# Agent attention with a gated convolution: one DMA transpose for a pair of units, and shifted rows copied as sixteen and three single rows

## The chip, the cores and the metric

The kernel runs on one core of a Trainium2 chip. A core has the engines PE (matmuls; its weight loads are listed as PEld), DVE, ACT and POOL (element-wise work), and SP, which here issues nearly all DMA transfers. Each engine executes its own instructions in order and waits on semaphores for the others. All transfers of the core are served by 16 DMA engines. The metric is the device time of one execution in microseconds (us); lower is better. The profile is of one execution and gives its span, from the first to the last instruction.

## The reference, cut to what matters

```python
# q, k, v: (4, 12800, 128); agents: (4, 49, 128)
def sm(a, b):                                   # row softmax of the scaled scores
    s = (a @ b.transpose(0, 2, 1)) / np.sqrt(128)
    e = np.exp(s - s.max(-1, keepdims=True))
    return e / (e.sum(-1, keepdims=True) + 1e-09)

x = sm(q, agents) @ (sm(agents, k) @ v)         # attention through 49 agents

gate_pre = sum(conv_w[t] * x_delayed_by(4 - t) for t in range(5))   # causal, per channel
gate = 1 / (1 + exp(-gate_pre))
out = (gate * (x @ w_val)) @ w_out
```

## The kernel before, in words

Each of the four batches has 12800 positions. They are worked in *units* of 1280 positions (10 a batch, 40 in all, numbered g) for keys, values and queries, and in *chunks* of 512 (25 a batch, 100 in all) for the gate, the value path and the output. Two units, an even one and the odd one behind it, make a *segment* of 2560 positions, which is five chunks. So there are 20 segments.

Keys and values of a batch give 49 agent values. `fold_weights` folds them into the convolution and value weights, so that gate and value of a chunk come out of matmuls whose contracted axis is the agents and whose moving operand is the softmax weights of the queries (`queries`), one row for each agent.

The softmax weights are held in 16 bits. To keep accuracy they are stored as rows of three kinds in `pt` (line 220), a tile of 128 positions by 10 blocks by 128 columns: 49 columns with the low part, 49 with the high part, and 30 that repeat the high part of two out of every three of the first 45 agents; these 30 meet the residuals of the folded weights. `queries` writes `pt` with ACT (line 779), POOL (line 784, the 30 repeated columns) and POOL again (line 794, the low parts). There are four `pt` tiles, used in turn.

A unit's `pt` has positions on partitions; the matmuls need agents there. `transposes` (line 827) turns it into one half of `x1`, a tile of 128 rows by one segment (four of them, with a few columns ahead of it that `halo`, line 813, copies from the segment before on POOL). The first four units are transposed on PE; the other 36 by one DMA transpose each, issued by SP (line 835).

The residuals of the 19 agents that are not repeated in `pt` need their high parts at all five delays. They are held in `x2` (line 222, three tiles): 19 agents by 5 delays are 95 rows, row by row a copy of an `x1` row shifted by 0 to 4 columns. `shifts` (line 866) makes these copies by two DMA transfers (line 884), cut by `X2CUTS` (line 36): 15 source rows, every third, to 75 rows of `x2`, and 4 neighbouring source rows to 20 more. The first four units have such copies each for themselves; from the fifth on they are made once for a segment, when both halves of `x1` are there. So there are 22 groups of copies, 44 transfers.

A chunk's gate (`gates`, line 898) is five matmuls on `x1` at five column offsets (line 922) and one on the 95 rows of `x2` (line 926), all into one accumulator, then a tanh on ACT. Its value (`values`, line 942) is one matmul on `x1` (line 949) and one on `x2` (line 953); then come the product on DVE (line 962) and its split into two 16-bit halves, `hh` on ACT and `hl` on POOL (line 973). `project` (line 979) has three matmuls (lines 992 to 994), the last of which needs `hl`, a scaled copy on ACT and the store.

Loads go through 11 buffers `ld` in the order of use, so they run ahead as far as buffers are free.

The order of the work is made in two ways. PE's sequence is written out by hand: the string `order` (k0.0, q0.0, g0, a0, ...). Everything else is put into order by `Plan` (lines 94 and on): each step is added with an engine, an estimated duration and what it reads and writes. The planner replays the program with these estimates, takes at each moment the ready step with the longest estimated way to the end, and issues all instructions in the order of the starting times found. For a DMA step it books the time of the issue, a time on the common wire (`moved`), and 1.4 us (`LAND`) until its result counts. SP's queue is in this order too, and so what stands ahead of a transfer on SP is settled by the planner. A transpose is booked with 1.4 us of issue and 2.4 us of wire; the copies with 0.6 us of issue and, for two units, 1.0 and 0.6 us of wire. Since each transfer waits on SP for its input, a transpose whose `pt` is not complete holds up what is behind it.

Of the kernel before, what the change touches and what calls it, by code (L numbers as in the profile page):

```python
# [10 lines left out]
F16 = mybir.dt.float16  # L11
# [21 lines left out]
THREES = 15  # L33
NDUP = 2 * THREES
X2R = 19
X2CUTS = ((0, THREES, 3, 0.5), (THREES, X2R, 1, 0.3))


NLOAD = 11
# [137 lines left out]
def tile_agent_attention_gated_conv(  # L177
# [91 lines left out]
    nc.vector.memset(x1s[0][:, 0:PAD], 0.0)  # L269
    for t in wst_sb:  # L270
        nc.gpsimd.memset(t[:, TAPS + 1 :, :], 0.0)

    moe_sb = const.tile([P, NW], F32, name="moe_sb")
    wval_sb = moe_sb[:, 0:C]
# [238 lines left out]
    def fold_weights(b):  # L513
# [57 lines left out]
        x2v = wst[:, TAPS + 2, 0 : TAPS * X2R].rearrange("p (r k) -> p k r", k=TAPS)  # L571
        ghi = wst[:, 0:TAPS, 0:A]
        vhi = wst[:, TAPS, 0:A]

# [12 lines left out]
        def val_weights():  # L587
            dve.tensor_reduce(
                out=mx[:, 1:2], in_=pv[:, 0:A], axis=AX.X, op=ALU.max,
                apply_absolute_value=True,  # L590
            )
            dve.tensor_scalar(
                out=mx[:, 1:2], in0=mx[:, 1:2], scalar1=TINY, scalar2=1.0 / WS,
                op0=ALU.max, op1=ALU.mult,
            )
            dve.reciprocal(out=rs[:, 1:2], in_=mx[:, 1:2])
            dve.tensor_scalar_mul(vhi, pv[:, 0:A], rs[:, 1:2])
            pv3, hi3 = threes(pv[:, 0:A]), threes(vhi)
            rest(
                wst[:, TAPS, 2 * A :].rearrange("p (i r) -> p i r", r=2),  # L600
                pv3[:, :, 0:2], 1, hi3[:, :, 0:2],
            )
            rest(x2v[:, HALO, 0:THREES], pv3[:, :, 2], 1, hi3[:, :, 2])
            rest(x2v[:, HALO, THREES:], pv[:, 3 * THREES : A], 1, vhi[:, 3 * THREES :])

        def gate_weights():
# [7 lines left out]
        def gate_rest_pool():  # L614
            def less(out, full, hi):
                nc.gpsimd.tensor_tensor(out=out, in0=full, in1=hi, op=ALU.subtract)

            gs3, hi3 = threes(gs), threes(ghi)
            twos = wst[:, 0:TAPS, 2 * A :].rearrange("p k (i r) -> p k i r", r=2)
            for r in range(2):  # L620
                less(twos[:, :, :, r], gs3[:, :, :, r], hi3[:, :, :, r])
            less(x2g[:, :, 0:THREES], gs3[:, :, :, 2], hi3[:, :, :, 2])
            less(x2g[:, :, THREES:], gs[:, :, 3 * THREES :], ghi[:, :, 3 * THREES :])

        def gate_rest():
            gw3, hi3 = threes(gw), threes(ghi)
            twos = wst[:, 0:TAPS, 2 * A :].rearrange("p k (i r) -> p k i r", r=2)
            for r in range(2):
                rest(twos[:, :, :, r], gw3[:, :, :, r], 0, hi3[:, :, :, r])
            rest(x2g[:, :, 0:THREES], gw3[:, :, :, 2], 0, hi3[:, :, :, 2])  # L630
            rest(x2g[:, :, THREES:], gw[:, :, 3 * THREES :], 0, ghi[:, :, 3 * THREES :])

        w_ = ("wst", x)
# [99 lines left out]
    def queries(b, u):  # L733
        g = b * NU + u
        x = g % 2
        i = slot_of["q", b, u]
        ps, at = bank()
        sT, d, e, w, r, sm = sts[x], qw[g % NPT], qw[g % NPT], qw[g % NPT], qr[x], qsm[x]
        pt = pts[g % NPT]
        sa = sT[:, :, 0:A]  # L740
        add("pe", 1.07, lambda: score_matmuls(b, ld[i], ps), [("ld", i), ("ld2", i)], [at], key="sc")
        add("dve", 0.84, lambda: transpose_blocks(sT, ps[:, :, 0:GT]), [at], [("sT", x)])
        add(
            "dve", 0.62,
            lambda: nc.vector.tensor_reduce(out=qmx[x], in_=sa, axis=AX.X, op=ALU.max),  # L745
            [("sT", x)], [("qmx", x)],
        )
        add(
            "pool", 1.05,
            lambda: nc.gpsimd.tensor_tensor(  # L750
                out=d, in0=sa, in1=qmx[x].unsqueeze(2).to_broadcast([P, NBLK, A]),
                op=ALU.subtract,
            ),
            [("sT", x), ("qmx", x)], [("qw", g % NPT)],
        )
# [12 lines left out]

        add("dve", 0.95, sums, [("qw", g % NPT)], [("qr", x)])
        add(  # L770
            "dve", 0.68,
            lambda: nc.vector.tensor_tensor(  # L772
                out=w, in0=e, in1=r.unsqueeze(2).to_broadcast([P, NBLK, A]), op=ALU.mult
            ),
            [("qw", g % NPT), ("qr", x)], [("qw", g % NPT)],
        )
        p_ = ("pt", g % NPT)
        add(
            "act", 0.58, lambda: nc.scalar.copy(out=pt[:, :, A : 2 * A], in_=w),  # L779
            [("qw", g % NPT)], [(*p_, 0)],  # L780
        )
# [45 lines left out]
    def transposes(b, u):  # L827
# [1 line left out]
        pt = pts[g % NPT]  # L829
        p_ = ("pt", g % NPT)  # L830
        if not on_pe(b, u):
            dst = unit_rows(g)
            add(
                "dma", 1.4,
                lambda: nc.sync.dma_start_transpose(
                    out=dst.rearrange("p (n i) -> p n i", i=P),
                    in_=pt.rearrange("p n r -> p (n r)"),
                ),
                [(*p_, n) for n in range(3)], [("x1", g // 2 % NX, g % 2)], 2.4,
            )  # L840
            shifts(b, u)
            return
# [23 lines left out]
    def shifts(b, u):  # L866

        g = b * NU + u
        if g >= SINGLE and g % 2 == 0:
            return  # L870
        n = 1 if g < SINGLE else 2
        u0 = u + 1 - n
        s = g // 2
        x2, x1 = x2s[s % 3], x1s[s % NX]
        o = (g + 1 - n) % 2 * UNIT
        src = row_keys(s, range(0, g % 2 + 1))
        c = PAD - HALO + o
        for r0, r1, every, us in X2CUTS:
            first = A + (2 if every == 3 else 3 * THREES)
            rows = x1[first : first + 1 + (r1 - r0 - 1) * every : every, c : c + 1]  # L880
            view = [rows.ap[0], (1, TAPS), (1, n * UNIT)]
            add(
                "dma", 0.6,
                lambda r0=r0, r1=r1, rows=rows, view=view: nc.sync.dma_start(
                    out=x2[r0 * TAPS : r1 * TAPS, o : o + n * UNIT],
                    in_=bass.AP(rows.tensor, rows.offset, view),
                ),
                src, [("x2", s % 3, o + i * UNIT, r0) for i in range(n)], us * n,
            )
        if g % 2 and (g + 1) // 2 < B * NU // 2:  # L890
            halo((g + 1) // 2)
# [6 lines left out]
    def gates(t):  # L898
# [20 lines left out]
        def matmuls():  # L919
            for k in range(TAPS):  # L920
                c = PAD - HALO + o2 + k
                nc.tensor.matmul(  # L922
                    out=pg, lhsT=stat[:, k, :], rhs=x1[:, c : c + w],
                    start=(k == 0), stop=False,
                )
            nc.tensor.matmul(  # L926
                out=pg, lhsT=stat[0 : TAPS * X2R, TAPS + 1, :],
                rhs=x2[0 : TAPS * X2R, o2 : o2 + w], start=False, stop=True,
            )

        th = ths[t % NT_][:, 0:w]
# [10 lines left out]
    def values(t):  # L942
# [5 lines left out]
        def matmuls():  # L948
# [2 lines left out]
                start=True, stop=False,  # L951
            )
            nc.tensor.matmul(  # L953
                out=pv, lhsT=stat[0 : TAPS * X2R, TAPS + 2, :],
                rhs=x2[0 : TAPS * X2R, o2 : o2 + w], start=False, stop=True,
            )

        h, hh, hl = hs[t % NH][:, 0:w], hhs[t % 3][:, 0:w], hls[t % 3][:, 0:w]
# [228 lines left out]
```

## Time and profile before

| | |
|---|---|
| device time, median of 3 runs | 427.45 us (426.17 to 427.92) |
| span of the profiled execution | 423.6 us |
| DMA moved | 127.62 MB, 75129 packets, mean 301 GB/s |
| transfers of line 884 | 18 of 375.0 KB and 18 of 100.0 KB (segments), 4 of 187.5 KB and 4 of 50.0 KB (first units) |
| transfers of line 835 | 36 DMA transposes |
| PE's matmuls | 3907 |

How to read the views quoted below: the page begins with busy time, share of the span and number of instructions of each engine, and later gives the shares of the chain that ended last. A row of a window has its limits in us from the span's start, its length, the busy time and number of instructions of PE, PEld, DVE, ACT and POOL, the granted PE clock as a share of full speed, the busy share of the DMA engines (it can pass 1, as packets overlap) and GB/s. A row of the waits says which engine and line waited for which other one: us in total, times, the longest. A row of a timeline has its start, its length, engine, line, operation and tiles (out<-in); x2 at its end or in a page row means a count, and a bracket tells how long the engine was idle before it and what ended that. For a transfer on SP the length is that of the issue on SP's sequencer, not of the transfer. Buffer numbers are left out of names, so x1 and x2 both stand as `x`, and x<-x is a copy of shifted rows. Matmuls are pipelined: their lengths overlap, and a new one of 512 columns starts every 0.22 us at full clock.

### The profile page before, as it was taken

To read this page: it belongs to the slowest core of one execution; us is meant where nothing else is said; L and a number is where in the kernel's file an instruction comes from. 1 tells how busy PE (TensorE), PEld (TensorE's weight loads), DVE (VectorE), ACT (ScalarE), POOL (GpSimd) and SP (SyncE) were. 2 spreads that over 40 slices of the span, in tenths; PEclk is the share of its full clock that TensorE was granted. 3 is DMA by queue.
4 is the path that set the end of the run, shared out by engine and by line. 5 is a ranking of instruction groups with operands and counts; after the bars stand their busy time and mean duration, and the time that the engine had idled before them with its cause. 6 is when DMAs were issued, how large, how long until landed. Compare 5 with 4: busy or idle time off the path is not lost.

```text
span 423.6 us, 10042 instructions
## 1 busy us (share of the span) xinstructions
PE 403.9 (95%) x3907; PEld 197.0 (47%) x3907; DVE 293.3 (69%) x562; ACT 301.5 (71%) x521; POOL 228.2 (54%) x263
## 2 busy tenths in 40 slices
PE   4979999999999999999999899999999989999995
PEld 1358434346555443446555343335555534344443
DVE  3757899867875978667795575767765678676231
ACT  1564568779966777678876486778876567788776
POOL 1002557654657565554566355574366277877553
PEclk9969999999999999999999899999999999999998
DMA  8999999999999999999999999999999977755733
GB/s 320 420 417 411 370 367 353 301 295 310 412 293 283 346 317 362 304 278 356 351 379 324 271 299 370 314 332 302 296 393 322 239 196 161 199 163 176 205 121 124
DMA packets 75129, 127.62 MB, mean 301 GB/s; under 512 B 50466, under 2 KB 50850, under 8 KB 75084
## 3 DMA queue, kind: packets, MB, share of 16 engines
q1 hardware_dynamic: 74940, 126.87, 96.9%
q8 instruction: 30, 0.49, 0.5%
q10 hardware_dynamic: 144, 0.13, 0.2%
q14 instruction: 15, 0.12, 0.1%
HBM read 79.25 MB, written 26.21 MB: 249 GB/s over the span
## 4 chain that ended last, share of the span: by engine, by line
PE 78%; DMA 9%; DVE 8%; ACT 1%; POOL 1%; issue 1%; SPq 0%; POOLq 0%; DVEq 0%; ACTq 0%
PE gate L922 23%; PE sc L376 17%; PE av L480 10%; PE val L949 5%; PE out L992 5%; PE val L953 5%; PE gate L926 5%; PE out L993 4%; DMA ld<-kT 4%; PE out L994 4%; DMA x<-pt 3%; DMA x<-x 2%; DVE h L962 1%; DVE qw L772 1%; DVE qsm L763 1%
## 5 line engine op out<-in xcount | busy, mean ns | idle before, releaser
L973 POOL TENSOR_TENSOR hl<-h,hh 128x512 f16<-128x512 f32 (+1 forms) x101 | 116.9, 1158 | 96.1 <-ACT hh L968 96.0
L922 PE MATMUL gate<-x,stat 128*128 128x512 f16 (+1 forms) x500 | 125.2, 380 | 0.2 <-ACT th L935 0.2
L962 DVE SCALAR_TENSOR_TENSOR h<-th,val 128x512 f32<-128x512 f32 x100 | 67.8, 678 | 66.8 <-PE out L993 26.2
L376 PE MATMUL sc<-ld,ag_sb 128*32 128x320 f32 x1280 | 101.5, 447 | 7.6 <-DMA ld<-kT 7.0
L935 ACT ACTIVATE th<-gate,unscale 128x512 f32<-128x512 f32 x100 | 68.3, 683 | 33.3 <-PE gate L926 31.7
L1006 ACT ACTIVATE ob<-out,oscale 128x512 f32<-128x512 f32 x98 | 67.3, 687 | 21.3 <-PE out L994 20.1
L922 PEld LDWEIGHTS <-stat 128*128 128x128 f16 x505 | 46.3, 97 | 63.7 <-issue 14.8
L968 ACT CAST hh<-h 128x512 f16<-128x512 f32 (+1 forms) x101 | 61.5, 609 | 17.2 <-DVE h L962 16.4
L750 POOL TENSOR_TENSOR qw<-sT,qmx 128x490 f32<-128x490 f32 x40 | 41.4, 1035 | 47.6 <-DVE qmx L745 47.5
L376 PEld LDWEIGHTS sc<-ld,ag_sb 128*32 128x32 f32 x1280 | 36.7, 111 | 59.4 <-issue 25.7
L480 PE MATMUL av<-ld,eT 128*32 128x129 f32 (+1 forms) x1400 | 50.7, 279 | 1.0 <-DVE eT L386 1.0
L480 PEld LDWEIGHTS av<-ld,eT 128*32 128x32 f32 (+1 forms) x1400 | 47.1, 117 | 7.5 <-issue 2.5
L794 POOL TENSOR_TENSOR pt<-qw,pt 128x490 f16<-128x490 f32 x40 | 44.8, 1120 | 3.1 <-ACT pt L779 2.9
L471 ACT ACTIVATE e<-ks,kbias 128x320 f32<-128x320 f32 x80 | 39.3, 554 | 5.4 <-DVE eT L386 3.3
L386 DVE STREAM_TRANSPOSE sT<-sc 128x640 f32<-128x640 f32 x40 | 33.6, 839 | 13.4 <-PE sc L376 12.7
L402 ACT COPY ks<-sc 128x640 f32<-128x640 f32 x40 | 27.7, 691 | 21.2 <-PE sc L376 19.1
L386 DVE STREAM_TRANSPOSE eT<-e 128x640 f32<-128x640 f32 x40 | 33.5, 842 | 9.8 <-ACT e L471 5.2
L926 PE MATMUL gate<-x,stat 95*128 95x512 f16 x100 | 38.3, 383 | 1.5 <-DMA x<-x 1.5
L949 PE MATMUL val<-x,stat 128*128 128x512 f16 x100 | 38.2, 382 | 0.8 <-DVE h L962 0.6
L953 PE MATMUL val<-x,stat 95*128 95x512 f16 x100 | 38.1, 381 | 0.0
L994 PE MATMUL out<-hl,wo 128*128 128x512 f16 x98 | 37.0, 378 | 1.1 <-POOL hl L973 1.1
L992 PE MATMUL out<-hh,wo 128*128 128x512 f16 x98 | 37.3, 381 | 0.1
(130 smaller groups left out, 389.4 us busy)
## 6 DMA issues: line engine op xcount, KB each, us to landing
ld<-kT SPq DMA_DIRECT2D x40, 640.0 KB
ld<-qT SPq DMA_DIRECT2D x40, 640.0 KB
ld<-vP SPq DMA_DIRECT2D x39, 645.0 KB
outT<-ob SPq DMA_DIRECT2D x48, 512.0 KB
x<-x SPq DMA_DIRECT2D x18, 375.0 KB
x<-x SPq DMA_DIRECT2D x18, 100.0 KB
outT<-ob SPq DMA_DIRECT2D x3, 256.0 KB
x<-x SPq DMA_DIRECT2D x4, 187.5 KB
```

The lines of the kernel that those rows point to most:

```text
L376: nc.tensor.matmul(out=out[g * BLK : (g + 1) * BLK, j, 0:GT], lhsT=ag_sb[:, b, j * BLK : (j + 1) * BLK], rhs=src[:, g * GT : (g + 1) * GT] ...
L386: nc.vector.transpose(out=out.rearrange("p n (j i) -> p j n i", j=2), in_=in_.rearrange("p j (n i) -> p j n i", i=BLK),)
L480: nc.tensor.matmul(out=av[o + j : o + j + cols, 0 : C + 1], lhsT=et[:, n, j : j + cols], rhs=vt[:, n, :], start=(u == 0 and n < 2), stop=( ...
L922: nc.tensor.matmul(out=pg, lhsT=stat[:, k, :], rhs=x1[:, c : c + w], start=(k == 0), stop=False,)
L926: nc.tensor.matmul(out=pg, lhsT=stat[0 : TAPS * X2R, TAPS + 1, :], rhs=x2[0 : TAPS * X2R, o2 : o2 + w], start=False, stop=True,)
L935: lambda: nc.scalar.activation(out=th, in_=pg, func=AF.Tanh, scale=unscale[:, 0:1]),
L949: nc.tensor.matmul(out=pv, lhsT=stat[:, TAPS, :], rhs=x1s[(b * NCH + n0 // CH) // 5 % NX][:, PAD + o2 : PAD + o2 + w], start=True, stop=False,
L953: nc.tensor.matmul(out=pv, lhsT=stat[0 : TAPS * X2R, TAPS + 2, :], rhs=x2[0 : TAPS * X2R, o2 : o2 + w], start=False, stop=True,)
L962: lambda: nc.vector.scalar_tensor_tensor(out=h, in0=th, scalar=1.0, in1=pv, op0=ALU.add, op1=ALU.mult),
L968: "act", 0.16 + 0.42 * scale, lambda: nc.scalar.copy(out=hh, in_=h),
L973: lambda: nc.gpsimd.tensor_tensor(out=hl, in0=h, in1=hh, op=ALU.subtract),
L1006: lambda: nc.scalar.activation(out=ob[:, o : o + w], in_=po, func=AF.Copy, scale=oscale),
```

## The change

The two `pt` tiles of a segment become the halves of one tile, and the even unit no longer has a transpose of its own: at the odd unit one DMA transpose takes both halves into the whole of `x1`. The planner books it with 2.6 us of issue and 3.6 us of wire. The roles of the agents are renumbered: the 30 repeated columns now belong to the second and third of every three agents, and the first of every three, with agents 45 to 48, goes to `x2`. In `x1` the source rows are thus 0, 3, ..., 45 (16 rows at an even distance) and 46, 47, 48. `X2CUTS` takes the 16 in one transfer and each of the last three in one of its own: four transfers for a group in place of two, 88 in all. `x2`'s rows start at partition 24, so they are 24 to 118; all of `x2` is set to zero once at the start by three memsets on POOL, and the two matmuls on `x2` contract over all 128 rows instead of 95. PE's written order is the same.

```diff
-X2CUTS = ((0, THREES, 3, 0.5), (THREES, X2R, 1, 0.3))
+X2O = 24
+X2CUTS = ((0, 16, 0, 3, 0.4), (16, 17, 46, 1, 0.05), (17, 18, 47, 1, 0.05), (18, 19, 48, 1, 0.05))
...
-    pts = ring(NPT, [P, NBLK, P], F16, "pt")
+    ptp = ring(NPT // 2, [P, 2, NBLK, P], F16, "pt")
+    pts = [t[:, h] for t in ptp for h in range(2)]
...
+    for t in x2s:
+        nc.gpsimd.memset(t, 0.0)
...
-        x2g = wst[:, TAPS + 1, 0 : TAPS * X2R].rearrange("p (r k) -> p k r", k=TAPS)
+        x2g = wst[:, TAPS + 1, X2O : X2O + TAPS * X2R].rearrange("p (r k) -> p k r", k=TAPS)
...
-                in0=w[:, :, 0 : 3 * THREES].rearrange("p n (i r) -> p n i r", r=3)[:, :, :, 0:2],
+                in0=w[:, :, 0 : 3 * THREES].rearrange("p n (i r) -> p n i r", r=3)[:, :, :, 1:3],
...
         if not on_pe(b, u):
-            dst = unit_rows(g)
+            if g % 2 == 0:
+                return
+            s = g // 2 % NX
+            pair = ptp[g // 2 % (NPT // 2)]
             add(
-                "dma", 1.4,
+                "dma", 2.6,
                 lambda: nc.sync.dma_start_transpose(
-                    out=dst.rearrange("p (n i) -> p n i", i=P),
-                    in_=pt.rearrange("p n r -> p (n r)"),
+                    out=x1s[s][:, PAD:].rearrange("p (n i) -> p n i", i=P),
+                    in_=pair.rearrange("p h n r -> p (h n r)"),
                 ),
-                [(*p_, n) for n in range(3)], [("x1", g // 2 % NX, g % 2)], 2.4,
+                [("pt", i % NPT, n) for i in (g - 1, g) for n in range(3)],
+                [("x1", s, 0), ("x1", s, 1)], 3.6,
             )
...
-        for r0, r1, every, us in X2CUTS:
-            first = A + (2 if every == 3 else 3 * THREES)
+        for r0, r1, agent, every, us in X2CUTS:
+            first = A + agent
...
-                    out=x2[r0 * TAPS : r1 * TAPS, o : o + n * UNIT],
+                    out=x2[X2O + r0 * TAPS : X2O + r1 * TAPS, o : o + n * UNIT],
...
-                out=pg, lhsT=stat[0 : TAPS * X2R, TAPS + 1, :],
-                rhs=x2[0 : TAPS * X2R, o2 : o2 + w], start=False, stop=True,
+                out=pg, lhsT=stat[:, TAPS + 1, :], rhs=x2[:, o2 : o2 + w],
+                start=False, stop=True,
```

The residual weights in `fold_weights` follow the new numbering in the same number of instructions, and the second matmul of `values` changes as the one shown here.

More of the change, by code (lines that the diff above doesn't have):

```diff
@@ L600, in val_weights @@
                 wst[:, TAPS, 2 * A :].rearrange("p (i r) -> p i r", r=2),
-                pv3[:, :, 0:2], 1, hi3[:, :, 0:2],
+                pv3[:, :, 1:3], 1, hi3[:, :, 1:3],
             )
-            rest(x2v[:, HALO, 0:THREES], pv3[:, :, 2], 1, hi3[:, :, 2])
+            rest(x2v[:, HALO, 0:THREES], pv3[:, :, 0], 1, hi3[:, :, 0])
             rest(x2v[:, HALO, THREES:], pv[:, 3 * THREES : A], 1, vhi[:, 3 * THREES :])
@@ L620, in gate_rest_pool @@
             for r in range(2):
-                less(twos[:, :, :, r], gs3[:, :, :, r], hi3[:, :, :, r])
-            less(x2g[:, :, 0:THREES], gs3[:, :, :, 2], hi3[:, :, :, 2])
+                less(twos[:, :, :, r], gs3[:, :, :, r + 1], hi3[:, :, :, r + 1])
+            less(x2g[:, :, 0:THREES], gs3[:, :, :, 0], hi3[:, :, :, 0])
             less(x2g[:, :, THREES:], gs[:, :, 3 * THREES :], ghi[:, :, 3 * THREES :])
@@ L628, in gate_rest @@
             for r in range(2):
-                rest(twos[:, :, :, r], gw3[:, :, :, r], 0, hi3[:, :, :, r])
-            rest(x2g[:, :, 0:THREES], gw3[:, :, :, 2], 0, hi3[:, :, :, 2])
+                rest(twos[:, :, :, r], gw3[:, :, :, r + 1], 0, hi3[:, :, :, r + 1])
+            rest(x2g[:, :, 0:THREES], gw3[:, :, :, 0], 0, hi3[:, :, :, 0])
             rest(x2g[:, :, THREES:], gw[:, :, 3 * THREES :], 0, ghi[:, :, 3 * THREES :])
@@ L953, in matmuls @@
             nc.tensor.matmul(
-                out=pv, lhsT=stat[0 : TAPS * X2R, TAPS + 2, :],
-                rhs=x2[0 : TAPS * X2R, o2 : o2 + w], start=False, stop=True,
+                out=pv, lhsT=stat[:, TAPS + 2, :], rhs=x2[:, o2 : o2 + w],
+                start=False, stop=True,
             )
```

2 lines of the change are left out of this document (1 added, 1 removed).

## The prediction, made before the changed kernel was run

> **What bounds the kernel now.** I read the page first (busy shares, chain), then the windows, then the waits of PE, and last the timelines of PE and of SP's queue around the few places where PE waits.
>
> ```profile
> span 423.6 us, 10042 instructions
> ...
> PE 403.9 (95%) x3907; PEld 197.0 (47%) x3907; DVE 293.3 (69%) x562; ACT 301.5 (71%) x521; POOL 228.2 (54%) x263
> ...
> PE 78%; DMA 9%; DVE 8%; ACT 1%; POOL 1%; issue 1%; SPq 0%; POOLq 0%; DVEq 0%; ACTq 0%
> ```
> ```profile
> 70.00:328.00 258.00, 256.42 (x2685) 123.26 (x2678) 188.21 (x348) 194.09 (x339) 149.53 (x165) 0.99 1.09 326
> 328.00:415.00 87.00, 85.14 (x542) 38.16 (x541) 52.44 (x104) 64.82 (x110) 55.48 (x60) 1.00 0.70 179
> ```
> ```profile
> PE out L994 <- POOL hl L973: 1.1, 1, 1.1
> ...
> PE gate L926 <- DMA x<-x: 1.5, 1, 1.5
> ```
> The chain is PE for 78%. In the window from 70 to 328 us PE is busy for 256.42 of 258 us and from 328 to 415 for 85.14 of 87, so in 345 us it has 3.4 us without a matmul. The next-to-last column is the DMA share: 1.09 up to 328, that is a queue with always something in it, and 0.70 behind it. So PE sets the end, and the transfers count only where their result comes late at PE. The waits name one such place for the tiles of this change: 1.5 us for a copy of shifted rows (x<-x).
>
> ```profile
> 232.93 1.24 PE L922 MATMUL gate<-x,stat 128*128 128x512 f16 x5
> 235.67 0.39 PE L926 MATMUL gate<-x,stat 95*128 95x512 f16 x1 [1.50 <-DMA x<-x]
> ...
> 236.89 2.24 PE L922 MATMUL gate<-x,stat 128*128 128x512 f16 x5
> ...
> 239.78 0.63 PE L953 MATMUL val<-x,stat 95*128 95x512 f16 x1
> ```
> The five matmuls on x1 run, the sixth (L926, on x2) waits 1.50 us, and the next five take 2.24 us where those before took 1.24; the last of their group still takes 0.63 instead of 0.38. Five starts lose 1.0 us, so the group's eight lose some 1.6. So a late x2 costs its wait and up to 1.6 us more. By the Trainium skill (TensorE: Matmul & The Clock Gate, section Part 1) the array falls back to half rate after an idle window of about 3.4 us; read so, a gap of 1.5 us should cost nothing beyond itself. The row here disagrees, and the sum goes by the row; by the rule the 1.6 us falls away from each rival below.
>
> **The change part by part.**
>
> *One transpose for two units.* 36 transposes become 18 of twice the size. What one costs depends on the stage.
>
> ```profile
> 361.24 2.94 SPq L835 DMA_TRANSPOSE x<-pt  x2
> ...
> 366.46 1.65 SPq L884 DMA_DIRECT2D x<-x  x2
> ...
> 376.80 1.35 SPq L835 DMA_TRANSPOSE x<-pt  x1
> ...
> 381.08 1.65 SPq L884 DMA_DIRECT2D x<-x  x2
> ```
> In the quiet stage a lone transpose takes SP 1.35 us, and the copies that wait for it go out 4.28 us after it (381.08 - 376.80). Two issued back to back take 2.94 us, and the copies follow 5.22 us after the first (366.46 - 361.24). A joined transpose has no row; its bounds are 4.28 us (it costs as one) and 5.22 us (as two in a row), and I take 5.2, the row with the same payload. It starts when the odd unit's tile is ready, as the second one did, so the copies move 0.9 us later. The cover there: those copies leave at 381.08, the chain below gives 7.34 us for landing in the worst stage, which is 388.4, and the use is
>
> ```profile
> 394.32 0.38 PE L926 MATMUL gate<-x,stat 95*128 95x512 f16 x1
> ```
> 5.9 us later. Nothing reaches PE.
>
> In the full stage the rows are these (SP's timeline, three segments of two units each, then the chain and PE's uses):
>
> ```profile
> 73.26 5.94 SPq L835 DMA_TRANSPOSE x<-pt  x1
> ...
> 79.94 2.68 SPq L835 DMA_TRANSPOSE x<-pt  x1
> ...
> 86.20 1.68 SPq L884 DMA_DIRECT2D x<-x  x2
> ```
> ```profile
> 114.65 9.57 SPq L835 DMA_TRANSPOSE x<-pt  x2
> ...
> 127.74 1.67 SPq L884 DMA_DIRECT2D x<-x  x2
> ```
> ```profile
> 212.77 7.23 SPq L835 DMA_TRANSPOSE x<-pt  x1
> 220.10 0.53 SPq L369 DMA_DIRECT2D ld<-kT  x1
> 220.73 2.63 SPq L835 DMA_TRANSPOSE x<-pt  x1
> ...
> 228.28 1.65 SPq L884 DMA_DIRECT2D x<-x  x2
> ```
> ```profile
> 220.73 7.50 DMA x<-pt
> 228.28 7.34 DMA x<-x
> ```
> ```profile
> 93.97 0.38 PE L926 MATMUL gate<-x,stat 95*128 95x512 f16 x1
> ```
> ```profile
> 135.69 0.38 PE L926 MATMUL gate<-x,stat 95*128 95x512 f16 x1
> ```
> The first transpose of a pair holds SP 5.94 or 7.23 us instead of 1.35: it stands behind transfers already queued, and the second goes out only when the first is through (79.20 to 79.94, 220.00 to 220.73). So where the queue is full the early start of the even unit gains little, and the pair lands together anyway; at 114.65 both are already issued in one stretch. What changes is what stands between them (the load at 220.10, for instance), which now goes ahead. The margins at PE, with 7.34 us for a copy's landing: 93.97 - 93.54 = 0.4 us in the segment at 94 us, 135.69 - 135.08 = 0.6 in that at 136, none in that at 236. Bounds for the shift of a joined transpose's landing here: -1.0 (the load between no longer splits the two) and, if it is issued no earlier than the second one was and takes what two took at 114.65 (13.09 us to the copies), 79.94 + 13.09 - 86.20 = +6.8. I take +0.5, near the queue's own logic (same transfers ahead, same payload), and 0 at 136.
>
> *Copies of shifted rows.* A group was two transfers (15 source rows, 375 KB; 4 rows, 100 KB) and becomes four (16 rows; three of one).
>
> ```profile
> L884 SPq DMA_DIRECT2D x<-x x44: 679/866/1132, 43.5 to 398.0; - x44
> L835 SPq DMA_TRANSPOSE x<-pt x36: 1352/3061/7234, 73.3 to 392.5; - x36
> ```
> 44 issues become 88. An added issue costs SP between 0 and 1.13 us; I take the least of the row, 0.68 (the small one), so +1.4 us of SP per group, 2.3 at most. Queued behind on SP are loads and stores. Neither is late at PE after 70 us, by the waits. The last small copy starts 1.4 us later than the old small one, but it carries a quarter of that one's bytes, so the landing moves less: bounds -0.5 and +1.4, taken 0.2. By the Trainium skill (DMA: Bandwidth & Descriptors, Rules for kernel authors) small transfers belong in one, since under 64 KB mostly overhead is paid: that speaks against three of 25 KB and for the +1.4 end, 1.2 us more at 94 and at 236. No row here has a copy so small. The first unit has it too:
>
> ```profile
> 43.52 1.83 SPq L884 DMA_DIRECT2D x<-x  x2
> ```
> ```profile
> 49.68 0.38 PE L926 MATMUL gate<-x,stat 95*128 95x512 f16 x1
> ```
> 6.16 us from issue to use, less than a full landing of 7.34, so this use has no margin: +0.2.
>
> *x2 in partitions 24 to 118, all 128 rows in its matmul.* Taken at nothing by the pair
>
> ```profile
> L949 PE MATMUL val<-x,stat 128*128 128x512 f16 x100 | 38.2, 382 | 0.8 <-DVE h L962 0.6
> L953 PE MATMUL val<-x,stat 95*128 95x512 f16 x100 | 38.1, 381 | 0.0
> ```
> 382 against 381 ns: rows don't cost. The zeroing of x2 is three memsets on POOL:
>
> ```profile
> 1.76 0.56 POOL L271 MEMSET wst<- 128x256 f16 x2
> 35.26 1.02 POOL L750 TENSOR_TENSOR qw<-sT,qmx 128x490 f32<-128x490 f32 x1 [32.94 <-DVE qmx L745]
> ```
> One of ten times the columns costs 0.3 to 3.1 us, three at most 9.4, in 32.94 us in which POOL is idle. The renumbered residual weights are the same instructions.
>
> *The order of the other engines.* The PE order is written out, but ACT, DVE, POOL and SP are laid out by the planner, and its numbers change: from the odd unit's tile to x2 it books 2.2 us more (a transpose 2.6 + 3.6 for 1.4 + 2.4, a copy 0.2 less). So it gives that chain 2.2 us more priority, where the real way is longer than booked (7.50 and 7.34 us for the two hops before 236). At 189 to 209 this has a visible handle:
>
> ```profile
> 189.28 0.66 DVE L772 TENSOR_TENSOR qw<-qw,qr 128x490 f32<-128x490 f32 x1
> ```
> ```profile
> 209.24 0.59 ACT L779 CAST pt<-qw 128x490 f16<-128x490 f32 x1
> ```
> The cast waits 19 us on ACT for other work, and the transpose of 212.77 waits for it. Bounds of the effect at 236: -3.1 (wait and slow stretch gone) to 0 or some loss elsewhere; I take -1.0.
>
> **Sum.** First unit +0.2; at 94 us 0.5 + 0.2 - 0.4 = +0.3; at 236 us +0.7 - 1.0 = -0.3, with the slow stretch staying; the rest 0: +0.2. 423.6 + 0.2 = 423.8 of span; the median of 427.45 is 3.85 us above the span, which I keep: **427.6 us**, no change that a measurement of this kernel can tell (0.5%, 2.1 us).
>
> **The rivals.**
>
> *Faster, the planner's larger booking.* The pair's tiles come 2 us or more earlier, x2 is there at 236, wait and slow stretch go: -3.1, 424.5; with POOL's halo copy laid out later, the 1.1 us at L994 goes too: 423.4. For it: that wait is the only one of PE on x2, its length is below the 2.2 us. Against: ACT work laid behind has users as well.
>
> ```profile
> 338.78 0.19 POOL L819 COPY x<-x 128x4 f16<-128x4 f16 x1 [5.99 <-DMA x<-pt]
> ```
> *Slower, the joined transpose comes late at a segment without margin.* SP is held by one issue of 9.57 us or more, and behind it stand the copies for PE; on POOL the halo copy (here 5.99 us) holds hl for L994. Place: 94 us, margin 0.4. Price: half of the upper bound, 3.4 us later, is 3.0 of wait and 1.6 of slow clock: 432.2; the full bound gives 435.6. It decides as soon as x2 lands more than 0.4 us later there. For it: three uses with margins under 0.7. Against: both halves already stand in one queue.
>
> *The change doesn't do what it says*, one issue being served as two and three small copies as one: 427.4.
>
> **Chances.** Forecast 0.38 and no effect 0.04: same 0.42. Faster by over 0.5% 0.31. Slower by over 0.5% 0.27. The range takes the faster case to 423.4 and the slower one to its price: 423.4 to 432.5; what lies beyond on both sides I put at 2 in 10.
>
> **What would show it.** The page should list 18 transposes and copies of 400 and 25 KB; SP's timeline, transposes of 2.7 to 3 us behind 350 us. If L926 waits for x<-x at 94 or 136, or L994 for hl by more than 1.1 us, the slower rival holds; if no L926 waits and no five of L922 take 2.2 us at 236, the faster one. A wait of PE on a load or on DVE and ACT that is not there now would mean that the new layout, which I can't see, decides, and all three are wrong.

## The result and the profile after

The changed kernel takes 439.53 us in the median (436.78 to 440.26) where the kernel before takes 426.81 beside it: a ratio of 1.028, 95% interval 1.0229 to 1.0332. It is 12.7 us slower; the prediction had 427.6 and a range up to 432.5. Some executions of a kernel come out over 1.5% slower than its fastest; the ratios in this document leave them out, the medians don't, and the profiled executions of join_replan and before_halo_later were such ones, so their traces are not read.

The page of the changed kernel, in the order in which the page of before was read: span, busy time, chain by engine.

```profile
span 438.2 us, 10051 instructions
...
PE 407.4 (93%) x3907; PEld 197.8 (45%) x3907; DVE 294.0 (67%) x562; ACT 300.3 (69%) x521; POOL 235.1 (54%) x266
...
PE 67%; DMA 20%; DVE 6%; issue 2%; SPq 2%; POOL 1%; ACT 1%; POOLq 0%; DVEq 0%
```

The span grew by 14.6 us (438.2 - 423.6). PE executes the same 3907 matmuls; its busy time is 3.5 us more, and the other 11.1 us are time in which it has none. In the chain DMA has 20% where it had 9%. The waits of PE in the changed kernel (line waited for, us in total, times, longest):

```profile
PE gate L934 <- DMA x<-x: 8.3, 3, 5.4
...
PE out L1002 <- POOL hl L981: 2.4, 2, 1.6
PE av L436 <- DVE m L429: 2.0, 1, 2.0
```

The waits for x2 (L934) were 1.5 us and are 8.3. The wait of L1002 for hl grew from 1.1 to 2.4. The wait of the key maximum's transpose (L436) for m, 2.0 us, had no counterpart at this place.

Since PE's order is written out and unchanged, the same matmul can be found in both timelines, and its delay can be followed. First the segment at 94 us, after:

```profile
94.02 1.24 PE L930 MATMUL gate<-x,stat 128*128 128x512 f16 x5
100.65 0.61 PE L934 MATMUL gate<-x,stat 128*128 128x512 f16 x1 [5.38 <-DMA x<-x]
...
145.18 0.38 PE L934 MATMUL gate<-x,stat 128*128 128x512 f16 x1
...
197.42 0.27 PE L436 MATMUL av<-ident,m 128*2 128x128 f32 x1 [2.02 <-DVE m L429]
...
248.87 0.39 PE L934 MATMUL gate<-x,stat 128*128 128x512 f16 x1 [2.69 <-DMA x<-x]
```

and the two rows of before that the prediction doesn't show:

```profile
92.90 1.24 PE L922 MATMUL gate<-x,stat 128*128 128x512 f16 x5
...
185.40 0.27 PE L432 MATMUL av<-ident,m 128*2 128x128 f32 x1
```

| matmul | before | after | delay |
|---|---|---|---|
| five on x1, segment at 94 us | 92.90 | 94.02 | 1.1 |
| on x2, same chunk | 93.97 | 100.65 | 6.7 |
| on x2, segment at 136 us | 135.69 | 145.18 | 9.5 |
| key maximum's transpose | 185.40 | 197.42 | 12.0 |
| on x2, segment at 236 us | 235.67 | 248.87 | 13.2 |
| end (span) | 423.6 | 438.2 | 14.6 |

So 1.1 us are lost ahead of this segment (not followed here), 5.6 (6.7 - 1.1) come from one wait at 94 us, the next 2.8 for the most part from the half clock behind it (the granted clock below), 2.0 of the next 2.5 from the wait for m, 1.2 from the segment at 236 us, and the rest behind it.

The window of the half clock in the changed kernel (busy us per engine, then granted clock, DMA share, GB/s):

```profile
99.88:106.71 6.83, 6.06 (x81) 4.01 (x85) 2.27 (x3) 3.77 (x8) 2.31 (x3) 0.50 1.04 290
```

Why x2 is late at 94 us is read from SP's timeline of the changed kernel:

```profile
79.39 2.70 SPq L373 DMA_DIRECT2D ld<-vP  x3
82.20 7.67 SPq L842 DMA_TRANSPOSE x<-pt  x1
...
92.02 3.01 SPq L892 DMA_DIRECT2D x<-x  x4
```

Before, the two transposes of this segment went out at 73.26 and 79.94 and the copies at 86.20. Now the one transpose goes out at 82.20, behind three loads, holds SP for 7.67 us, and the copies go out at 92.02, 5.8 us later than before. It is not its data that it waits for: POOL's last write to the second tile of the pair ends at 77.76 (76.67 + 1.09), 4.4 us earlier.

```profile
76.67 1.09 POOL L798 TENSOR_TENSOR pt<-qw,pt 128x490 f16<-128x490 f32 x1
```

Why the key maximum is late is read from POOL's timeline, then ACT's (in the square brackets: idle before, and what ended it):

```profile
190.42 0.19 POOL L823 COPY x<-x 128x4 f16<-128x4 f16 x1 [6.07 <-DMA x<-pt]
190.57 1.02 POOL L754 TENSOR_TENSOR qw<-sT,qmx 128x490 f32<-128x490 f32 x1
```
```profile
191.62 0.61 ACT L762 ACTIVATE qw<-qw 128x490 f32<-128x490 f32 x1 [3.73 <-POOL qw L754]
...
194.52 0.69 ACT L406 COPY ks<-sc 128x640 f32<-128x640 f32 x1
```

POOL stands 6.07 us in the halo copy, which reads what the transpose of the segment before has written. Behind it on POOL is qw; ACT waits 3.73 us for that; behind ACT's exponential are the copies of the key scores, from which the maximum m is made. A copy of four columns thus reaches PE over three engines. Before, the halo copy ahead of that matmul waited for no transfer:

```profile
180.02 0.19 POOL L819 COPY x<-x 128x4 f16<-128x4 f16 x1 [0.47 <-issue]
```

### The profile page after: what moved, and what is told of

It reads as the page before. It is cut to its first block, busy times and chain, and to the rows that moved or that the text cites. A ratio compares the mean times of both kernels' runs of the same rounds, so it can differ in the third digit from the quotient of the medians.

```text
span 438.2 us, 10051 instructions
## 1 busy us (share of the span) xinstructions
PE 407.4 (93%) x3907; PEld 197.8 (45%) x3907; DVE 294.0 (67%) x562; ACT 300.3 (69%) x521; POOL 235.1 (54%) x266
## 4 chain that ended last, share of the span: by engine, by line
PE 67%; DMA 20%; DVE 6%; issue 2%; SPq 2%; POOL 1%; ACT 1%; POOLq 0%; DVEq 0%
PE gate L930 19%; PE sc L380 15%; PE av L484 9%; DMA x<-pt 7%; DMA x<-x 5%; DMA ld<-kT 4%; DMA ld<-vP 4%; PE val L957 4%; PE gate L934 4%; PE out L1000 4%; PE val L961 4%; PE out L1001 4%; PE out L1002 4%; SPq L892 1%; DVE h L970 1%
## 5 line engine op out<-in xcount | busy, mean ns | idle before, releaser
L380 PE MATMUL sc<-ld,ag_sb 128*32 128x320 f32 x1280 | 104.5, 457 | 8.7 <-DMA ld<-kT 7.9
L934 PE MATMUL gate<-x,stat 128*128 128x512 f16 x100 | 38.3, 383 | 8.3 <-DMA x<-x 8.3
L957 PE MATMUL val<-x,stat 128*128 128x512 f16 x100 | 38.2, 382 | 1.5 <-DVE h L970 1.3
L1002 PE MATMUL out<-hl,wo 128*128 128x512 f16 x98 | 37.1, 379 | 2.4 <-POOL hl L981 2.4
L961 PE MATMUL val<-x,stat 128*128 128x512 f16 x100 | 38.0, 380 | 0.0
```

The lines of the kernel that those rows point to most:

```text
L380: nc.tensor.matmul(out=out[g * BLK : (g + 1) * BLK, j, 0:GT], lhsT=ag_sb[:, b, j * BLK : (j + 1) * BLK], rhs=src[:, g * GT : (g + 1) * GT] ...
L934: nc.tensor.matmul(out=pg, lhsT=stat[:, TAPS + 1, :], rhs=x2[:, o2 : o2 + w], start=False, stop=True,)
L957: nc.tensor.matmul(out=pv, lhsT=stat[:, TAPS, :], rhs=x1s[(b * NCH + n0 // CH) // 5 % NX][:, PAD + o2 : PAD + o2 + w], start=True, stop=False,
L961: nc.tensor.matmul(out=pv, lhsT=stat[:, TAPS + 2, :], rhs=x2[:, o2 : o2 + w], start=False, stop=True,)
```

## The experiments

Three theories of the whole (the expectations below name those of each run A and B anew). **The layout**: the changed bookings make the planner lay out ACT, DVE, POOL and SP anew, and that costs more than the transfers do. **The join**: the joined transpose, long on SP and waiting for the second unit, is the loss. **The copies**: the four copies are.

| run | transposes | copies | order | us | ratio to before (95%) |
|---|---|---|---|---|---|
| after | joined | 16,1,1,1 | new | 439.53 | 1.0280 (1.0229 to 1.0332) |
| join_oldorder | joined | 15,4 | before's | 431.87 | 1.0112 (1.0064 to 1.0160) |
| copies_oldorder | separate | 16,1,1,1 | before's | 424.86 | 0.9941 (0.9914 to 0.9967) |
| both_oldorder | joined | 16,1,1,1 | before's | 432.70 | 1.0124 (1.0065 to 1.0184) |
| two_neworder | two back to back | 16,1,1,1 | after's | 439.08 | 1.0263 (1.0215 to 1.0312) |
| join_replan | joined | 15,4 | new | 438.57 | 1.0190 (1.0162 to 1.0218) |
| copies_replan | separate | 16,1,1,1 | new | 431.10 | 1.0085 (1.0056 to 1.0113) |
| halo_later | joined | 16,1,1,1 | after's, halo later | 434.26 | 1.0170 (1.0142 to 1.0197) |
| turn_first | joined | 16,1,1,1 | after's, transposes first | 438.99 | 1.0292 (1.0246 to 1.0339) |
| turn_halo | joined | 16,1,1,1 | halo later, transposes earlier | 431.83 | 1.0139 (1.0099 to 1.0179) |
| two_copies_oldorder | separate | 16,3 | before's | 426.67 | 1.0017 (0.9995 to 1.0038) |
| copies_halo_later | separate | 16,1,1,1 | before's, halo later | 422.35 | 0.9911 (0.9881 to 0.9941) |
| both_halo_later | joined | 16,1,1,1 | before's, halo later | 429.52 | 1.0059 (1.0032 to 1.0086) |
| two_back_to_back_oldorder | two back to back | 16,1,1,1 | before's, halo later | 428.23 | 1.0013 (0.9980 to 1.0047) |
| copies_replan_halo | separate | 16,1,1,1 | new, halo later | 432.69 | 1.0106 (1.0062 to 1.0149) |
| before_halo_later | separate | 15,4 | before's, halo later | 422.58 | 0.9879 (0.9845 to 0.9914) |

The experiments were run in four batches, each beside the kernel before (426.8, 427.3, 426.9 and 427.5 us in the median), so across batches the ratios are the better measure.

**The parts, each in before's order.** The planner's bookings stay those of before, so ACT, DVE and POOL keep their order and only the transfers differ. The edit for the joined transpose (the even unit's step issues nothing):

```diff
-                lambda: nc.sync.dma_start_transpose(
-                    out=dst.rearrange("p (n i) -> p n i", i=P),
-                    in_=pt.rearrange("p n r -> p (n r)"),
-                ),
+                lambda: joined(g) if g % 2 else None,
```

> The joined transpose alone, in the order of the kernel before: the planner's steps and bookings are those of before, the even unit's transpose step issues nothing, and the odd unit's step issues the joined one. ACT, DVE and POOL keep their order of before instruction by instruction. Theory 'order' (the new layout that the planner makes from the new bookings is what costs): within 0.5% of before, 425 to 429 us. Theory 'joining' (one issue of twice the size lands later, whatever stands around it): most of the 12.7 us, 434 us or more, with the wait of the x2 matmul at about 94 us several us long.

> The copies alone, in the order of before: sixteen rows in the first copy step's place and the three single rows in the second's, x2 in partitions 24 to 118, separate transposes with their bookings of before. Theory 'order': within 0.5% of before. Theory 'copies' (44 more issues on SP delay what is behind): 430 us or more, with x2 landing over 1 us later at 94 and 236 us.

> All the transfers of the change in the order of before. Theory 'order': within 0.5% of before, and so 10 us faster than the change. If joining and copies cost by themselves, the sum of their two losses.

The join costs 1.1% (431.87 us, between the ranges of its two theories), the copies gain 0.6%, and both together cost 1.2%. The new order, the only thing in which after differs from both_oldorder, takes it from 1.012 to 1.028. The copies as transfers are out as a cause; the join and the layout each hold a part.

The late x2 at 94 us belongs to the layout more than to the join. With the same transfers in before's order (both_oldorder, SP and then PE) the copies go out at 86.99, 5.0 us earlier than in after and 0.8 later than before, and PE waits 0.83 us there instead of 5.38:

```profile
77.64 7.30 SPq L834 DMA_TRANSPOSE x<-pt  x1
...
86.99 2.90 SPq L893 DMA_DIRECT2D x<-x  x4
```
```profile
95.80 0.38 PE L935 MATMUL gate<-x,stat 128*128 128x512 f16 x1 [0.83 <-DMA x<-x]
```

**The one long issue or the waiting.** The order of after, but two transposes issued one behind the other where the joined one stands:

```diff
+            def two():
+                for h in range(2):
+                    o = PAD + h * UNIT
+                    nc.sync.dma_start_transpose(
+                        out=x1s[s][:, o : o + UNIT].rearrange("p (n i) -> p n i", i=P),
+                        in_=pair[:, h].rearrange("p n r -> p (n r)"),
+                    )
```

> The changed kernel with its order, where the step of the joined transpose issues two transposes of one unit each, back to back; the rest is as in the change. Theory 'order': as slow as the change, 437 to 441 us. Theory 'joining' as a matter of one large issue: clearly faster than the change, 433 us or less.

439.08 against 439.53: no difference that shows. In this order one transpose of two units costs what two in a row do.

**The planner with one part of the change at a time.** join_replan is before with the joined transpose and its bookings (2.6 and 3.6); copies_replan is after with the separate transposes of before (1.4 and 2.4).

> Before's kernel with the change's joined transposes and their bookings (2.6 and 3.6 us), the planner free to lay the steps out anew; the copies of shifted rows stay two (15 and 4 rows). Theory A (the new bookings of the transposes move the other engines' steps, and that costs some 7 us beside the 5 us of the join itself): 436 to 440 us, with a wait of PE for x2 of over 3 us near 94 us or waits behind POOL's halo copy. Rival B (the loss beyond the join comes from the bookings of the four copies): 430 to 433 us, as the join in the order of before (431.9).

> The changed kernel with the two separate transposes of before, booked as before (1.4 and 2.4 us each), its four copies of shifted rows with their bookings, and the planner free. Theory A (the copies' bookings are harmless): 424 to 427 us, as the same copies in the order of before (424.9). Rival B (four steps on SP's queue instead of two move the loads and the other engines' steps): 430 us or more.

The join goes from 1.011 to 1.019 by its bookings, the copies from 0.994 to 1.009 by theirs. So the copies' bookings are not harmless, and the join's are not alone: either set gives a layout worse than before's, by 0.8% and 1.4%. The 0.8% is the weaker of the two: the ratio of join_replan rests on two executions (434.59 and 435.70 us, between the ranges of its two theories), and the intervals barely part.

**What in the new layout costs.** halo_later moves only POOL's halo copies, turn_first only the joined transposes on SP:

```diff
-    for i in plan.order():
+    line = plan.order()
+    for s, i in halo_at.items():
+        if s in turn_at:
+            line.remove(i)
+            line.insert(line.index(turn_at[s]) + 1, i)
+    for i in line:
         plan.steps[i][2]()
```

> The changed kernel with POOL's halo copies moved back in the order written out: each stands right behind the issue of its own segment's transpose, where the transpose that it reads landed long ago. Theory A (POOL waits 6 us in the halo copy, and the steps behind it, the products qw and the low parts hl, make ACT, the key maxima at 197 us and the output at 315 us late): the waits of 2.0 us for m and 1.6 us for hl are gone, 434 to 437 us. Rival B (those steps were late for another reason and the halo copy is only where POOL's spare time lies): 438.5 to 440.5 us.

> The changed kernel with each joined transpose moved forward on SP's queue, right behind the last step that it depends on, ahead of the loads that the planner had put before it. Theory A (the wait of 5.4 us for x2 near 94 us, and the half clock behind it, come from the three loads of v on SP ahead of the transpose): that wait falls to under 2 us, 431 to 435 us. Rival B (the loads that now come behind the transposes are late, and PE waits for them instead): 437 us or more, with a wait of PE for a load that isn't there now.

The halo copy counts: 434.26 us, 5.3 less than after (1.1% by the ratios), and in the waits of PE for halo_later the 2.0 us for m and the waits of the output for hl of over 1 us are gone:

```profile
PE gate L938 <- DMA x<-x: 10.7, 3, 5.9
...
PE sc L1006 <- POOL hl L985: 0.4, 1, 0.4
```

What stays is x2, 10.7 us in three waits. (That the halo copy is no fault of the new layout alone is seen further down.) turn_first gains nothing (438.99), but not for the reason of its rival: no wait for a load appears that could pay for it (0.9 us for the loads of v, all before 40 us). SP's timeline of turn_first:

```profile
78.73 6.58 SPq L844 DMA_TRANSPOSE x<-pt  x1
...
88.10 0.97 SPq L895 DMA_DIRECT2D x<-x  x1
89.16 7.61 SPq L844 DMA_TRANSPOSE x<-pt  x1
96.81 2.13 SPq L895 DMA_DIRECT2D x<-x  x3
```
```profile
102.17 0.59 PE L937 MATMUL gate<-x,stat 128*128 128x512 f16 x1 [8.63 <-DMA x<-x]
```

The transpose does go out 3.5 us earlier (78.73 against 82.20) and the first copy 3.9 us earlier, but my edit also put the next segment's transpose between the first copy and the other three, which had to wait 7.6 us for SP. So this run shows what one joined transpose ahead of a copy costs (the wait at PE grew to 8.63 us), and leaves its own question open. turn_halo asks it again, with the transposes kept behind the copies of the segment before, and with the later halo copies:

> As halo_later (the changed kernel with later halo copies), with each joined transpose also moved forward on SP, ahead of the loads, but behind the last copy of shifted rows of the segment before it, so that it doesn't split a group of copies as in turn_first. Theory A (x2 of the segment near 94 us is late because its transpose is issued late): that transpose goes out near 77 us, PE's wait for x2 there falls from 3.9 to under 1.5 us, 429 to 432 us. Rival B (the joined transpose holds SP longer the earlier it is issued, and lands no sooner): 433.5 to 436 us.

431.83 us is in theory A's range, but its interval overlaps that of halo_later, the transpose went out only 1.4 us earlier (78.09 against 79.49), and PE's wait at that place was 2.76 us, not under 1.5. The earlier transposes' worth isn't settled.

**The later halo copy in before's order.**

> As copies_oldorder, with POOL's halo copies moved back behind the issue of their own segment's second transpose. Theory A (POOL's 16 us of waiting in the halo copy reach PE by the 1.5 us for hl alone): 422.5 to 424.5 us. Rival B (nothing of it reaches the end): 424.5 to 425.5 us.

> As both_oldorder (all transfers of the change in before's order), with POOL's halo copies behind the issue of their own segment's transpose. Theory A (of the join's 5 us in the old order some 2 come by way of the halo copy on POOL, the rest by x2 landing late at PE): 429.5 to 431.5 us, and the waits of PE for hl under 0.5 us. Rival B (the halo copy matters only in the planner's new order): 432 to 433.5 us.

> As both_halo_later (four copies, before's order, later halo copies), but instead of the one joined transpose two separate ones, issued one behind the other where the joined one stood. Theory A (the join's 7 us is the waiting of the first unit's transpose for the second unit's tile): 428 to 431 us, as both_halo_later (429.5). Rival B (it is the one long issue that holds SP): 422 to 425 us, as copies_halo_later (422.35).

> The kernel before, with POOL's halo copies behind the issue of their own segment's second transpose, nothing else changed. Theory A (the later halo copy is worth the same 2.5 us with the old copies): 423.5 to 425.5 us. Rival B (it is worth something only beside the four copies): 426 to 427.5 us.

With POOL out of the way in all of them, the join takes 0.991 to 1.006, 7.2 us by the medians (422.35 to 429.52). Two issues back to back give 1.001: putting the first unit's issue where the second's stands costs some 1.0% by itself, and what the one long issue adds (0.5%) lies within overlapping intervals. Where the later start costs is seen at 236 us. SP and then PE with separate transposes (copies_halo_later):

```profile
215.19 7.27 SPq L843 DMA_TRANSPOSE x<-pt  x1
222.55 0.53 SPq L374 DMA_DIRECT2D ld<-kT  x1
223.19 2.62 SPq L843 DMA_TRANSPOSE x<-pt  x1
...
229.37 3.05 SPq L893 DMA_DIRECT2D x<-x  x4
```
```profile
234.14 1.24 PE L931 MATMUL gate<-x,stat 128*128 128x512 f16 x5
236.78 0.38 PE L935 MATMUL gate<-x,stat 128*128 128x512 f16 x1 [1.40 <-DMA x<-x]
```

and with the joined one (both_halo_later):

```profile
219.56 10.48 SPq L837 DMA_TRANSPOSE x<-pt  x1
...
233.76 3.44 SPq L897 DMA_DIRECT2D x<-x  x4
```
```profile
233.75 1.24 PE L935 MATMUL gate<-x,stat 128*128 128x512 f16 x5
240.84 0.59 PE L939 MATMUL gate<-x,stat 128*128 128x512 f16 x1 [5.85 <-DMA x<-x]
```

The separate first transpose goes out at 215.19 and holds SP for 7.27 us; the second then needs SP for 2.62. The joined one goes out at 219.56, in the second one's place behind the loads, and does all of its standing in the queue from there. The copies leave 4.4 us later (233.76 - 229.37), and PE, which comes to this place at the same time, waits 5.85 us instead of 1.40.

It is the place on SP and not the second unit's data that makes the joined one late here, against the wording of theory A: POOL's last write to the second tile (the twentieth of this line, for unit 19) ends at 215.52 in copies_halo_later and at 215.04 in both_halo_later, 4.5 us before the joined transpose goes out:

```profile
215.07 0.45 POOL L789 TENSOR_SCALAR pt<-qw 128x300 f16<-128x300 f32 x1
```
```profile
214.59 0.45 POOL L789 TENSOR_SCALAR pt<-qw 128x300 f16<-128x300 f32 x1
```

before_halo_later answers what the later halo copy is worth by itself: 1.2% (422.58 us, more than its theory A asked), as fast as copies_halo_later, whose interval overlaps; these two beat both kernels of the case. So with the halo copy out of the way the four copies gain nothing that shows, and the halo copy cost before about as much (4.9 us, 427.51 to 422.58) as it cost after (5.3). By these two differences it is no part of what the change added, though after's trace shows it so plainly. Before's waits of PE name only 1.1 us of it (L994); how the rest reaches the end isn't shown. Nor is the move worth the same everywhere: with the four copies in before's order it gives 0.3% and with all transfers of the change 0.7%, both with overlapping intervals, and in the next run nothing.

> As copies_replan (separate transposes, four copies, the planner free), with POOL's halo copies behind the issue of their own segment's second transpose. Theory A (what the new order costs is POOL standing in the halo copy): 423 to 426 us. Rival B (the new order brings x2 to PE late by SP's queue, whatever POOL does): 428.5 to 432 us, with waits of PE for x2 of over 5 us in sum.

432.69 us: rival B, just above its range, and no gain over copies_replan (431.10). With the same transfers as copies_halo_later, and the halo copies as late, the planner's layout alone costs 1.9% by the ratios, some 8 us (10.3 by the medians, which are of two batches). PE waits for x2 in two places:

```profile
PE gate L934 <- DMA x<-x: 11.7, 2, 9.7
```

The larger one is at 236 us, where SP's timeline has, against 215.19, 223.19 and 229.37 in copies_halo_later:

```profile
221.63 7.79 SPq L842 DMA_TRANSPOSE x<-pt  x1
...
230.14 2.60 SPq L842 DMA_TRANSPOSE x<-pt  x1
...
238.54 3.32 SPq L892 DMA_DIRECT2D x<-x  x4
```

The first transpose leaves 6.4 us later and the copies 9.2 us later. The tiles are there in time: POOL's last write to the second one ends at 216.14, only 0.6 us later than in copies_halo_later. That is the layout's price at this place: not another wait on POOL, but the chain to x2 put later on SP. Four pairs differ in the layout only; by the ratios it costs 1.6% (after and both_oldorder), 1.4% (copies_replan and copies_oldorder), 1.1% (halo_later and both_halo_later) and 1.9% (copies_replan_halo and copies_halo_later). So it is some 5 to 8 us whatever is transferred. Which of the planner's choices puts the chain later wasn't tried.

**The number of small copies.**

> As copies_oldorder (before's transposes and order of steps, x2 in the middle partitions), but the three copies of one source row are one copy of three rows: two transfers of 16 and 3 rows. Theory A (the gain of 0.6% comes from the copy of 16 rows, whose issue takes 0.68 us and not 0.92, or from the layout; the three single rows only cost SP 0.65 us each): 423.5 to 425 us. Rival B (the three single copies land sooner than one of several rows, and that is the gain): 426 to 427.5 us, as before.

One copy of three rows in place of three of one gives 1.0017, no gain over before, where three single ones gave 0.9941. So theory A of that run (the 16-row copy or the layout) falls. Why three small issues are better there isn't shown; with the halo copy later the gain isn't there.

## Why the prediction was wrong

**What bounds the kernel** was right: PE sets the end, and the whole loss is PE waiting at a few places, and the half clock behind them.

**The joined transpose.** Its quiet price was right: copies 5.1 us behind it, where 5.2 was predicted from two in a row.

```profile
407.46 3.15 SPq L842 DMA_TRANSPOSE x<-pt  x1
412.53 3.27 SPq L892 DMA_DIRECT2D x<-x  x4
```

Under load it was mis-sized: taken at +0.5 us of landing, with bounds of -1.0 and +6.8. At 236 us the copies behind it went out 4.4 us later than behind separate ones in the paired runs above, and 2.6 later in the pair without the later halo copy (230.79 in both_oldorder, 228.23 in copies_oldorder). Over the whole kernel, in before's order, the join costs 1.1% alone, 1.8% beside the four copies and 1.5% beside these and the later halo copy, some 5 to 8 us. The step that failed is the sentence "So where the queue is full the early start of the even unit gains little, and the pair lands together anyway". The rows of 212.77 and 220.73, quoted beside it, show the opposite when read by what each issue costs: the early one takes the 7.23 us of standing in the queue, and the later one only 2.63. At 94 us, where the sum priced it, the size was about right in before's order: the copies go out 0.8 us later (86.99 against 86.20), where it had 0.5 + 0.2; most of after's 5.8 us there came with the layout.

**The order of the other engines** was as large an error, and with the wrong sign. The step read "So it gives that chain 2.2 us more priority", took -1.0 us, and left the "some loss elsewhere" without a price. Measured (after against both_oldorder), the new layout costs 6.8 us by the medians, and in four pairs 5 to 8. With more booked for the chain, x2 came later and not earlier: at 94 us the copies went out at 92.02 in after and at 86.99 in both_oldorder.

**The slow clock** was priced at 1.6 us for a late x2. At 94 us it was 6.83 us at 0.50, of which the delays above make at most 2.8 us. Its place was right, its length not.

**The copies.** Predicted +0.2 and a little of SP; measured -2 us (0.6%) in before's order and nothing beside a later halo copy. SP's time per group did grow, by 1.3 us at 94 us (3.01 for 1.68), and no wait of PE for a load came of it. The rule cited from the Trainium skill (DMA: Bandwidth & Descriptors, Rules for kernel authors), that small transfers belong in one, isn't borne out here: three of 25 KB were not slower than one of 75 KB.

**The rows of x2's matmul and the memsets**: nothing, as predicted; L934 takes 383 ns where L926 took 383.

```profile
L934 PE MATMUL gate<-x,stat 128*128 128x512 f16 x100 | 38.3, 383 | 8.3 <-DMA x<-x 8.3
```

**The rivals.** The slower one named the place (94 us), a late x2, hl behind the halo copy and two signs, and all of these came true in after; but it took half of its own upper bound (the issue of 9.57 us that it names is a row of two issues), and its cause was only part of it: at 94 us the same joined transpose in before's order costs PE 0.83 us, so what made x2 late there was mostly the layout. The sentence on new waits applied as well: L436 waiting for DVE wasn't there, and it meant that the layout decides. The faster rival assumed that a larger booking brings the chain forward; it fell with that step. Its other part, "POOL's halo copy laid out later", is worth far more than the 1.1 us it was given, and has nothing to do with the change.

## What to carry to other kernels

Two transfers in a full queue are not one transfer of their sum: the early one does its standing in line before the later one's turn comes, and joining them gives that start away, so price the join from the first issue's long duration and not from the landing of the pair. Where a planner lays out the engines, change the bookings and the transfers in separate runs; here the layout cost as much as the transfers it was booked for, or more. And look for small instructions that stand in an in-order engine on something far away: moving a copy of four columns was worth 1.2% of the kernel before, more than any part of the change gained, though in other orders less or nothing.

## What the runs showed of the hardware

The granted clock falls in steps of one length. In the changed kernel it was 0.50 from 99.88 to 106.71 and again here:

```profile
250.07:253.48 3.41, 3.40 (x10) 1.15 (x9) 2.07 (x7) 1.19 (x2) 1.71 (x2) 0.50 1.15 246
```

3.41 us and 6.83, twice that, and the two starts are 150.19 us apart, which is 44 times 3.413. In before it was 3.42 us, behind a window of the same length in which PE was busy for 1.91 us:

```profile
233.57:236.98 3.41, 1.91 (x11) 1.02 (x10) 1.10 (x4) 1.43 (x3) 0.53 (x1) 1.00 1.26 190
236.98:240.40 3.42, 3.42 (x9) 1.18 (x9) 2.01 (x7) 1.30 (x2) 1.84 (x3) 0.50 1.05 335
```

By the Trainium skill (TensorE: Matmul & The Clock Gate, Part 1) activity is judged over a free-running window of 3413 ns; the trace agrees with that grid. It doesn't agree that a whole window must be idle: the wait of 1.50 us before 235.67 was enough in before, while in turn_halo a wait of 2.76 us at 96 us was followed by a full clock:

```profile
96.57 0.39 PE L939 MATMUL gate<-x,stat 128*128 128x512 f16 x1 [2.76 <-DMA x<-x]
```
```profile
91.79:95.20 3.41, 1.90 (x9) 0.58 (x6) 2.26 (x3) 2.72 (x6) 1.15 (x1) 1.00 1.10 322
95.20:98.62 3.42, 2.05 (x41) 1.28 (x45) 0.38 (x1) 1.56 (x4) 0.29 (x1) 1.00 1.10 214
```

The grid tells most of the difference. In turn_halo a half clock began at 23.52, and 21 steps of 3.413 us behind it, at 95.20, a line of the grid cuts this wait in two: 1.5 us without a matmul in one window (3.41 - 1.90) and 1.4 in the next (3.42 - 2.05). Over the 15 traces read here, from 42 to 415 us, every window of the grid at full clock with more than 2.0 us without a matmul (13 of them) was followed by the half clock, 4 of the 19 with 1.5 to 2.0 us were, and none with less. So the idle share of a window decides but for a narrow band; what decides within the band isn't shown. The same late x2 can therefore cost its wait alone or, as at 94 us in after, up to 2.8 us more.
